# Thresholded attention with a feed-forward layer: sending the thresholds of the first eight pairs through DRAM, with an eighth score buffer and new planner ranks

## The chip, the cores and the metric

The kernel runs on one core of one Trainium2 chip. Its engines are TensorE (PE in the profile, with PEld for weight loads), VectorE (DVE), ScalarE (ACT), GpSimd (POOL) and SyncE (SP), which here only issues DMAs. The metric is the device time of one execution in microseconds; less is better. A change counts as faster or slower from 2%.

## The reference, cut to what matters

```python
# q, k, v: (8 batches, 8 heads, 576 positions, 64); tau = 0.02
scores = scale * np.matmul(q, k.transpose(0, 1, 3, 2))
thresh = np.max(scores, axis=-1, keepdims=True) - tau
scores = np.where(scores >= thresh, scores, -1e9)
attn = softmax(scores)                 # with 1e-9 added to the sum
x = (attn @ v) as (4608 tokens, 512)
h = x @ w_in                           # 512 -> 2048
out = (h * sigmoid(1.702 * h)) @ w_out # 2048 -> 512
```

The weights arrive as 8-byte floats, and the kernel turns them into 4-byte ones itself, in 32 pieces of 0.5 MB, each loaded twice.

## The kernel before

Two heads of one batch are a pair; there are 32. Keys lie on the partitions and queries along the row, so the maximum over keys is taken across partitions. DVE does this in steps: maxima over groups of 32 rows, then over tiles, then over groups. What is left are 2 x 576 = 1152 thresholds, lying as 32 partitions x 36 numbers. The kernel spreads them over 128 partitions (1377 ns) before it subtracts them:

```python
    def lower(n):                       # thresholds of pair n
        f = work.tile([P, 2 * QB], FP32, name="thr", tag="thr")
        nc.vector.tensor_scalar(out=f[0:32], in0=stats[n, ALU.max][0:32],
            scalar1=scl[0:32], scalar2=tau_b[0:32], op0=ALU.mult, op1=ALU.subtract)
        for w in (32, 64):
            nc.vector.tensor_copy(out=f[w : 2 * w], in_=f[0:w])
        stats[n, ALU.max] = f

    def spread_max(n):                  # every threshold on all partitions
        mb = home(n, "mb", 2 * S, "mb", 1)
        nc.vector.transpose(
            out=mb, in_=stats[n, ALU.max].unsqueeze(2).to_broadcast([P, 2 * QB, 32]))
        ...
    def sub(n, t):                      # score * scale - threshold
        ...
            nc.vector.scalar_tensor_tensor(
                out=s, in0=s, scalar=scl, in1=mb, op0=ALU.mult, op1=ALU.subtract)
        ...                             # the tail tile: two such, 64 partitions each
    def exps(n, t):
        nc.scalar.activation(out=s, in_=s, func=AF.Exp, bias=shift)
```

The order of instructions on each engine is made while the kernel is built: every piece of work is a task with an engine, a cost, a rank and a lag until its result can be used, and a planner in the kernel runs them through these figures. The engines then keep to that order and wait where a result is late: DVE's instructions up to 130 us, 131 of them in the trace of the change, stand in the same order in e1 below, with 66.5 us of waits on thresholds in one and 24.1 in the other. A wrong cost gives no wrong result (e4 changes two and is correct), only an order that does not fit the chip.

## Time and profile before

| | before |
|---|---|
| time, median | 1448.8 us (3 runs), 1447.7 with a fourth beside the change |
| profiled span | 1446.5 us |
| PE busy | 1384.0 us |
| DVE busy | 997.7 us |
| last wait of PE | ends at 292.6 us |

PE is the engine that sets the end. It has holes only before 293 us, while DVE is full there; the prediction shows these lines. Two lines that it leans on without showing them come from the page's list of loads (bytes of one issue, then the median time from issue to landing) and from the groups of instructions (count, busy time, mean ns, idle before):

```profile
k_raw<-in_k_dram SPq DMA_DIRECT2D x116, 72.0 KB, 2.3
```

```profile
L411 ACT ACTIVATE s_m<-s_m,shift 128x1152 f32<-128x1152 f32 x120 | 150.2, 1252 | 2.5
```

The first is a load of 576 runs of 128 bytes that lands 2.3 us after the start of its issue (landing times are counted from there throughout). The second is the exponential on a main tile. Two more measurements of this trace, for the prediction. After PE's wait of 9.7 us its granted clock was 0.50 until 29 us and 1.00 from 30 us, and the first three groups of eight matmuls took 2.19, 2.17 and 1.45 us instead of 1.14 to 1.19, about 2.3 us more in all; the same count gives 3.1, 1.6 and 2.8 us after the waits of 4.0, 7.2 and 10.5 us. After the one of 9.4 us the clock was 0.50 until 295.6 us, about 1.5 us lost (an estimate from that clock). And with the weight pieces on their way, the DMA moved 387 to 430 GB/s between 26 and 36 us.

### The profile page before, as it was taken

How to read it: one execution, taken by the hardware profiler on the slowest of the kernel's cores; microseconds unless marked ns; L12 is line 12 of the kernel's file. 1: busy time of each engine (PE TensorE's matmuls, PEld its weight loads, DVE VectorE, ACT ScalarE, POOL GpSimd, SP SyncE). 2: the span in 40 equal slices, each digit the busy share in tenths (PEclk: the TensorE clock that was granted, in tenths of full speed). 3: DMA queues.
4: the chain of work that ended last, by engine and by line, in shares of the span. 5: the costliest groups of instructions: out<-in, count | busy, mean ns of one | idle time of the engine just before them, and what ended most of it. 6: DMA issues, size and time to landing. Idle time of an engine off the chain costs nothing.

```text
span 1446.5 us, 13628 instructions
## 1 busy us (share of the span) xinstructions
PE 1384.0 (96%) x4936; PEld 650.1 (45%) x4936; DVE 997.7 (69%) x1650; ACT 643.6 (44%) x885; POOL 1.3 (0%) x13
## 2 busy tenths in 40 slices
PE   5769979899999999999999999999999999999998
PEld 3334434344444444444444444444444444444443
DVE  7998998888978888888878886788777820200100
ACT  5675544555545554555555554455445500100100
POOL 0000000000000000000000000000000000000000
PEclk8879999999999999999999999999999999999999
DMA  8239461111122012211111111111110000000000
GB/s 240 49 130 287 146 251 40 40 25 25 27 44 49 15 29 39 47 32 25 25 40 39 25 25 39 40 25 21 32 36 16 1 7 22 0 7 22 0 7 22
DMA packets 205074, 72.18 MB, mean 50 GB/s; under 512 B 192208, under 2 KB 192208, under 8 KB 205008
## 3 DMA queue, kind: packets, MB, share of 16 engines
q1 hardware_dynamic: 202640, 71.03, 19.1%
q8 instruction: 39, 0.64, 0.2%
q10 hardware_dynamic: 2368, 0.30, 0.1%
q14 instruction: 27, 0.22, 0.1%
HBM read 61.85 MB, written 9.44 MB: 49 GB/s over the span
## 4 chain that ended last, share of the span: by engine, by line
PE 88%; DVE 8%; ACT 1%; DMA 1%; issue 1%; DVEq 0%; ACTq 0%; SPq 0%
PE ops L523 33%; PE hps L504 31%; PE pv L425 11%; PE ps L319 9%; PE ps L312 2%; PE den L425 2%; DVE part L352 1%; DVE s_m L394 1%; DMA w64s<-in_moe_w_out_dram 1%; DVE mb L386 1%; DVE gT L515 0%; DVE w_out L284 0%; DVE w64s L276 0%; DVE part_t L352 0%; ACT s_m L338 0%
## 5 line engine op out<-in xcount | busy, mean ns | idle before, releaser
L523 PE MATMUL ops<-w_out,gT 128*128 128x512 f32 x1152 | 507.0, 597 | 7.4 <-DVE w_out L284 7.3
L504 PE MATMUL hps<-xT,w_in 128*128 128x512 f32 x1152 | 507.6, 596 | 1.5 <-DVE gT L515 1.4
L352 DVE TRANSPOSE_TENSOR_REDUCE part<-s_m 128x36 f32<-128x1152 f32 x228 | 301.3, 1355 | 107.4 <-ACT s_m L338 106.5
L523 PEld LDWEIGHTS ops<-w_out,gT 128*128 128x128 f32 x1152 | 217.7, 191 | 278.6 <-issue 265.7
L504 PEld LDWEIGHTS hps<-xT,w_in 128*128 128x128 f32 x1152 | 215.3, 190 | 274.2 <-issue 244.4
L515 DVE SCALAR_TENSOR_TENSOR gT<-th,hps 128x512 f32<-128x512 f32 x144 | 97.2, 675 | 226.4 <-ACT th L512 225.8
L338 ACT COPY s_m<-ps 128x576 f32<-128x576 f32 x240 | 137.2, 657 | 144.5 <-PE ps L319 143.3
L407 ACT ACTIVATE s_m<-s_m 128x1152 f32<-128x1152 f32 x120 | 138.4, 1153 | 119.7 <-DVE s_m L394 119.6
L512 ACT ACTIVATE th<-hps 128x512 f32<-128x512 f32 x144 | 85.3, 592 | 229.6 <-PE hps L504 229.5
L394 DVE SCALAR_TENSOR_TENSOR s_m<-s_m,scl,mb 128x1152 f32<-128x1152 f32 x120 | 163.3, 1411 | 0.6
L319 PE MATMUL ps<-qkT 64*128 64x288 f32 x960 | 141.8, 433 | 17.3 <-DVE qkT L295 17.3
L411 ACT ACTIVATE s_m<-s_m,shift 128x1152 f32<-128x1152 f32 x120 | 150.2, 1252 | 2.5
L425 PE MATMUL pv<-s_m,v_m 128*64 128x288 f32 x960 | 126.2, 414 | 0.0
L319 PEld LDWEIGHTS ps<-qkT 64*128 64x128 f32 x960 | 83.2, 190 | 89.4 <-issue 40.4
L530 ACT ACTIVATE osb<-ops 128x512 f32<-128x512 f32 x36 | 21.3, 591 | 220.4 <-PE ops L523 220.4
L425 PEld LDWEIGHTS pv<-s_m,v_m 128*64 128x64 f32 x960 | 67.5, 139 | 64.2 <-issue 15.0
L400 DVE SCALAR_TENSOR_TENSOR s_t<-s_t,scl,mb 64x576 f32<-64x576 f32 x60 | 48.7, 812 | 0.4
L492 DVE TENSOR_TENSOR xT<-pv,rc 128x288 f32<-128x288 f32 (+8 forms) x96 | 28.4, 351 | 22.4 <-PE pv L425 21.1
L352 DVE TRANSPOSE_TENSOR_REDUCE part_t<-s_t 128x18 f32<-128x576 f32 x59 | 43.7, 741 | 0.0
L386 DVE STREAM_TRANSPOSE mb<-thr 128x1152 f32<-128x1152 f32 x30 | 41.3, 1377 | 0.9
L312 PE MATMUL ps<-qkT,kd 128*128 128x288 f32 x120 | 37.1, 432 | 0.0
L425 PE MATMUL pv<-s_t,v_t 128*64 128x288 f32 x256 | 36.5, 406 | 0.0
(66 smaller groups left out, 571.1 us busy)
## 6 DMA issues: line engine op xcount, KB each, us to landing
out_dram<-osb SPq DMA_DIRECT2D x36, 256.0 KB, 2.0
q_raw<-in_q_dram SPq DMA_DIRECT2D x120, 72.0 KB, 2.3
k_raw<-in_k_dram SPq DMA_DIRECT2D x116, 72.0 KB, 2.3
v_m<-in_v_dram SPq DMA_DIRECT2D x64, 128.0 KB, 2.4
w_out<-in_moe_w_in_dram SPq DMA_DIRECT2D x12, 512.0 KB, 6.5
w<-in_moe_w_out_dram SPq DMA_DIRECT2D x12, 512.0 KB, 5.0
w_out<-in_moe_w_in_dram SPq DMA_DIRECT2D x12, 511.6 KB, 7.4
w64s<-in_moe_w_out_dram SPq DMA_DIRECT2D x12, 511.6 KB, 6.0
```

Source lines behind the costliest of these rows:

```text
L312: nc.tensor.matmul(ps[:, i, 0:SH], lhsT=kd[n % 2], rhs=qT[:, ts(i, SH)], start=True, stop=True,)
L319: nc.tensor.matmul(ps[:, h, 0:SH], lhsT=kT[ts(h, D), ts(t, P)], rhs=qT[ts(h, D), ts(c, SH)], start=True, stop=True,)
L338: nc.scalar.copy(out=o, in_=pss.pop((n, t, c))[:, :, 0:SH])
L352: nc.vector.tensor_reduce(out=o, in_=i, axis=AXL.X, op=op, apply_transpose=True)
L394: nc.vector.scalar_tensor_tensor(out=s, in0=s, scalar=scl, in1=mb, op0=ALU.mult, op1=ALU.subtract)
L407: nc.scalar.activation(out=s, in_=s, func=AF.Prelu, alpha=STEEP)
L411: nc.scalar.activation(out=s, in_=s, func=AF.Exp, bias=shift)
L425: nc.tensor.matmul(o[c][ts(h, D), 0:SH], lhsT=lhsT, rhs=rhs, start=(t == 0), stop=(t == NKT),)
L504: nc.tensor.matmul(hidden[j], lhsT=w_in[:, c, ts(j, P)], rhs=xTs[blk][:, c, :], start=(c == 0), stop=(c == NDC - 1),)
L512: nc.scalar.activation(out=ths[j], in_=hidden[j], func=AF.Tanh, scale=GELU_SCALE / 2)
L515: nc.vector.scalar_tensor_tensor(out=gT[j], in0=ths.pop(j), scalar=1.0, in1=hidden.pop(j), op0=ALU.add, op1=ALU.mult)
L523: nc.tensor.matmul(acc[i], lhsT=gT[j][:, ts(i, P)], rhs=w_out[:, j, :], start=(j == 0), stop=(j == NFC - 1),)
```

## The change

The intent is to take work off DVE while DVE holds everything up. For the first eight pairs the 1152 thresholds go to DRAM and come back spread over the partitions by the DMA. The scale moves into the exponential, so that the subtraction becomes a plain one. An eighth buffer of scores and ranks by kind of task let two pairs alternate, so that there is other work while a threshold travels.

```diff
+    EARLY = {"lower": -1.16, "values": 0.42, "exps": 0.63, "load_qk": -0.91, "prep": -1.45}
+    LATER = {"in_groups": 1.11}
     def task(engine, cost, rank, f, *a, after=(), take=(), give=(), lag=0.06):
+        if 0 <= rank < LAST:
+            rank += (EARLY if a[0] < 2 * NPAIR else LATER).get(f.__name__, 0.0)
 ...
     def lower(n):
-            out=f[0:32], in0=stats[n, ALU.max][0:32], scalar1=scl[0:32],
-            scalar2=tau_b[0:32], op0=ALU.mult, op1=ALU.subtract,
-        for w in (32, 64):
+            out=f[0:32], in0=stats[n, ALU.max][0:32], scalar1=gap[0:32], scalar2=None,
+            op0=ALU.subtract,
+        for w in (32, 64) if n >= BY_DMA else ():
 ...
+    def row_out(n):
+        rows[n] = dram.tile([1, 2 * S], FP32, name="row", tag="row", bufs=2)
+        nc.sync.dma_start(
+            out=rows[n].rearrange("o (c i) -> i (o c)", i=32), in_=stats[n, ALU.max][0:32])
+    def row_in(n):
+        ...
+        nc.sync.dma_start(out=mb, in_=row.to_broadcast([P, 2 * S]))
+        for h in range(2):
+            nc.sync.dma_start(out=mbt[ts(h, D)], in_=row[:, ts(h, S)].to_broadcast([D, S]))
 ...
     def sub(n, t):
-            nc.vector.scalar_tensor_tensor(
-                out=s, in0=s, scalar=scl, in1=mb, op0=ALU.mult, op1=ALU.subtract)
+            nc.vector.tensor_tensor(out=s, in0=s, in1=mb, op=ALU.subtract)
+        elif n in mbts:
+            nc.vector.tensor_tensor(out=s, in0=s, in1=mbts.pop(n), op=ALU.subtract)
 ...
-        nc.scalar.activation(out=s, in_=s, func=AF.Exp, bias=shift)
+        nc.scalar.activation(out=s, in_=s, func=AF.Exp, scale=scl, bias=shift)
 ...
+    BY_DMA = 8
 ...
+        if n < BY_DMA:
+            a = task("SP", 0.5, r, row_out, n, after=[a], take=("row",), lag=2.4)
+            m = task("SP", 1.4, r, row_in, n, after=[a], ..., lag=3.2)
```

(Cut: s_m buffers 7 to 8 and, to make room, io 3 to 2 and others by one; tau loaded by GpSimd's queue; one early exponential so that its table is loaded first; adjusted planner costs; ranks of the weight loads.)

More of the change, by code (lines that the diff above doesn't have):

```diff
@@ L22 @@
 EPS = 1e-9
+BIG = 3.0e38
 STEEP = 1.0e30
@@ L79 @@
     work = ctx.enter_context(tc.tile_pool(name="work", bufs=2))
+    dram = ctx.enter_context(
+        tc.tile_pool(name="dram", bufs=2, space=bass.MemoryType.DRAM)
+    )
     psA = ctx.enter_context(tc.tile_pool(name="psA", bufs=3, space=bass.MemoryType.PSUM))
@@ L92 @@
     tau_b = const.tile([P, 1], FP32, name="tau_b")
+    neg = const.tile([P, 1], FP32, name="neg")
     scl = const.tile([P, 1], FP32, name="scl")
+    gap = const.tile([P, 1], FP32, name="gap")
     shift = const.tile([P, 1], FP32, name="shift")
     tasks = []
-    limits = {"psA": 3, "psM": 2, "s_m": 7, "s_t": 2, "io": 3, "xT": 3, "mb": 1,
-              "raw0": 1, "raw1": 1, "qkT0": 1, "qkT1": 1, "v_m": 2, "w64": 2}
+    limits = {"psA": 3, "psM": 2, "s_m": 8, "s_t": 2, "io": 2, "xT": 3, "mb": 1,
+              "raw0": 1, "raw1": 1, "qkT0": 1, "qkT1": 1, "v_m": 2, "w64": 2, "mbt": 1, "row": 2}
     for x in ("raw0", "raw1", "qkT0", "qkT1", "mb"):
@@ L110, in task @@
         return len(tasks) - 1
+    FIRST, LAST = -9.0, 1000.0
     def run_in_order():
@@ L287, in cv_end @@
         )
-    mats, sT, stats, mbs, pss = {}, {}, {}, {}, {}
+    mats, sT, stats, mbs, mbts, rows, pss = {}, {}, {}, {}, {}, {}, {}
     def prep(n, which):
@@ L331, in keep @@
             if c == 0:
-                st = home(n, "s_m", 2 * S, "s_m", 7, f"s_m{t}")
+                st = home(n, "s_m", 2 * S, "s_m", 8, f"s_m{t}")
                 st = st.rearrange("p (h s) -> p h s", h=2)
@@ L344, in in_groups @@
                 work.tile([P, NKT, 2 * QB], FP32, name="part", tag="part", bufs=2),
-                work.tile([P, QB], FP32, name="part_t", tag="part_t", bufs=3),
+                work.tile([P, QB], FP32, name="part_t", tag="part_t", bufs=2),
             ]
@@ L356, in over_tiles @@
         pm, pt = stats[n, op]
-        r = work.tile([P, 2 * QB], FP32, name="red", tag="red", bufs=3)
+        r = work.tile([P, 2 * QB], FP32, name="red", tag="red", bufs=2)
         nc.vector.tensor_reduce(
@@ L367, in over_groups @@
         r = stats[n, op]
-        o = work.tile([64, 2 * QB], FP32, name="fold", tag="fold")
+        o = work.tile([64, 2 * QB], FP32, name="fold", tag="fold", bufs=1)
         for w in (64, 32):
@@ L389, in spread_max @@
         mbs[n] = mb.rearrange("p (h s) -> p h s", h=2)
+    def row_out(n):
+        rows[n] = dram.tile([1, 2 * S], FP32, name="row", tag="row", bufs=2)
+        nc.sync.dma_start(
+            out=rows[n].rearrange("o (c i) -> i (o c)", i=32), in_=stats[n, ALU.max][0:32]
+        )
+    def row_in(n):
+        mb = home(n, "mb", 2 * S, "mb", 1)
+        mbt = work.tile([P, S], FP32, name="mbt", tag="mbt", bufs=1)
+        row = rows.pop(n)
+        nc.sync.dma_start(out=mb, in_=row.to_broadcast([P, 2 * S]))
+        for h in range(2):
+            nc.sync.dma_start(out=mbt[ts(h, D)], in_=row[:, ts(h, S)].to_broadcast([D, S]))
+        mbs[n] = mb.rearrange("p (h s) -> p h s", h=2)
+        mbts[n] = mbt
     def sub(n, t):
@@ L393, in sub @@
         if t < NKT:
-            nc.vector.scalar_tensor_tensor(
-                out=s, in0=s, scalar=scl, in1=mb, op0=ALU.mult, op1=ALU.subtract
-            )
+            nc.vector.tensor_tensor(out=s, in0=s, in1=mb, op=ALU.subtract)
+        elif n in mbts:
+            nc.vector.tensor_tensor(out=s, in0=s, in1=mbts.pop(n), op=ALU.subtract)
         else:
             for h in range(2):
-                x = s[ts(h, D)]
-                nc.vector.scalar_tensor_tensor(
-                    out=x, in0=x, scalar=scl[ts(h, D)], in1=mb[ts(h, D), h, :],
-                    op0=ALU.mult, op1=ALU.subtract,
+                nc.vector.tensor_tensor(
+                    out=s[ts(h, D)], in0=s[ts(h, D)], in1=mb[ts(h, D), h, :], op=ALU.subtract
                 )
@@ L473, in spread_sums @@
         nc.vector.reciprocal(out=r, in_=r)
-        rc = work.tile([P, S], FP32, name="rc", tag="rc")
+        rc = work.tile([P, S], FP32, name="rc", tag="rc", bufs=1)
         nc.vector.transpose(out=rc, in_=r.unsqueeze(2).to_broadcast([P, QB, 32]))
@@ L510, in tanh @@
     def tanh(j):
-        ths[j] = work.tile([P, BLK], FP32, name="th", tag="io", bufs=3)
+        ths[j] = work.tile([P, BLK], FP32, name="th", tag="io", bufs=2)
         nc.scalar.activation(out=ths[j], in_=hidden[j], func=AF.Tanh, scale=GELU_SCALE / 2)
@@ L528, in half @@
     def half(i):
-        osbs[i] = work.tile([P, d_model], FP32, name="osb", tag="io", bufs=3)
+        osbs[i] = work.tile([P, d_model], FP32, name="osb", tag="io", bufs=2)
         nc.scalar.activation(out=osbs[i], in_=acc.pop(i), func=AF.Copy, scale=0.5)
@@ L536 @@
     NP = B * NPAIR
-    nc.sync.dma_start(
-        out=tau_b, in_=bass.AP(tensor=tau.tensor, offset=tau.offset, ap=[[0, P], [1, 1]])
-    )
+    nc.gpsimd.memset(rebias, -896.0 * 2.0**23)
     for t in kd + v_t + [ones_t]:
@@ L543, with first_act @@
     nc.gpsimd.memset(ones, 1.0)
-    nc.gpsimd.memset(rebias, -896.0 * 2.0**23)
     for h in range(2):
         nc.gpsimd.memset(ones_t[ts(h, D), h, :], 1.0)
+    nc.gpsimd.dma_start(
+        out=tau_b, in_=bass.AP(tensor=tau.tensor, offset=tau.offset, ap=[[0, P], [1, 1]])
+    )
+    def first_act():
+        nc.scalar.activation(out=neg, in_=rebias, func=AF.Exp)
     def tau_terms():
+        nc.vector.tensor_single_scalar(out=neg, in_=tau_b, scalar=0.0, op=ALU.is_lt)
         nc.vector.tensor_scalar(
-            out=scl, in0=tau_b, scalar1=0.0, scalar2=SCALE, op0=ALU.is_ge, op1=ALU.mult
+            out=scl, in0=neg, scalar1=-SCALE, scalar2=SCALE, op0=ALU.mult, op1=ALU.add
         )
@@ L558, in tau_terms @@
         nc.vector.tensor_single_scalar(out=shift, in_=tau_b, scalar=-1.0, op=ALU.mult)
-    FIRST, LAST = -1.0, 1000.0
+        nc.vector.tensor_single_scalar(out=gap, in_=tau_b, scalar=1.0 / SCALE, op=ALU.mult)
+        nc.vector.scalar_tensor_tensor(
+            out=gap, in0=neg, scalar=BIG, in1=gap, op0=ALU.mult, op1=ALU.add
+        )
     BY_PE = 5
+    BY_DMA = 8
     LEAD = 6
@@ L568 @@
     for i in range(len(pieces)):
-        rank = NPAIR - 0.4 + 0.5 * i / n_in if i < n_in else NPAIR - 0.16 + 0.9 * (i / n_in - 1)
+        rank = 4.36 + 0.21 * i / n_in if i < n_in else 4.6 + 0.19 * (i / n_in - 1)
         if not wide:
@@ L575 @@
         a = task("SP", 1.1, rank, load_w, i, take=place, lag=5.0)
-        e = task("DVE", 0.44, rank, cv_ex, i, after=[a])
-        m = task("ACT", 0.72, rank, cv_power, i, after=[e])
+        e = task("DVE", 0.43, rank, cv_ex, i, after=[a])
+        m = task("ACT", 0.79, rank, cv_power, i, after=[e])
         a = task("DVE", 1.14, rank, cv_frac, i, after=[e])
         over = [ready_w[y] for y in range(i) if i >= n_in and stage(y) == (i - n_in) // PER_STAGE]
-        ready_w.append(task("DVE", 0.72, rank, cv_end, i, after=[a, m] + over, give=place))
-    tau_done = task("DVE", 1.0, -2.0, tau_terms)
+        ready_w.append(task("DVE", 0.7, rank - 0.47, cv_end, i, after=[a, m] + over, give=place))
+    warm = task("ACT", 1.5, -2.0, first_act)
+    tau_done = task("DVE", 1.0, -2.0, tau_terms, after=[warm])
     placed, ffn = {}, []
@@ L598, in feed_forward @@
                 ffn.append(task(
-                    "PE", 1.79, LAST, mm1, blk, j, p, after=after,
+                    "PE", 1.762, LAST, mm1, blk, j, p, after=after,
                     take=("psM",) if p == 0 else (), give=("xT",) if last else (),
@@ L603, in feed_forward @@
             gelus[j] = task(
-                "DVE", 0.7, FIRST, gelu, j, after=[a, last_mm2.get(j // 2)],
+                "DVE", 0.69, FIRST, gelu, j, after=[a, last_mm2.get(j // 2)],
                 give=("psM", "io"),
@@ L613, in feed_forward @@
                 ffn.append(task(
-                    "PE", 1.79, LAST, mm2, i, p, after=after, take=("psM",) if p == 0 else (),
+                    "PE", 1.762, LAST, mm2, i, p, after=after, take=("psM",) if p == 0 else (),
                 ))
@@ L628 @@
         r = float(n)
+        slow = 1.2 if n < NPAIR else 1.0
         q0, q1 = (nc.sync, nc.scalar) if n == 0 else (nc.sync, nc.sync)
@@ L632 @@
         lv = task("SP", 2.1, r - 1.2, load_v, n, take=("v_m",), lag=2.0)
-        pq = task("DVE", 0.78, r, prep, n, 0, after=[lq], take=own(n, "qkT0"), give=own(n, "raw0"))
-        pk = task("DVE", 0.78, r, prep, n, 1, after=[lk], take=own(n, "qkT1"), give=own(n, "raw1"))
+        pq = task("DVE", 0.77, r, prep, n, 0, after=[lq], take=own(n, "qkT0"), give=own(n, "raw0"))
+        pk = task("DVE", 0.77, r, prep, n, 1, after=[lk], take=own(n, "qkT1"), give=own(n, "raw1"))
         pd = task("ACT", 0.5, r, prep_kd, n, after=[pk])
@@ L642 @@
                 a = task(
-                    "PE", 1.1 if tail else 0.58, r, scores, n, t, c,
+                    "PE", (0.97 if tail else 0.53) * slow, r, scores, n, t, c,
                     after=[pq, pk] + ([pd] if tail else []) + after,
@@ L648 @@
                 after = [a]
-                copies.append(task("ACT", 0.64, r, keep, n, t, c, after=[a], give=("psA",)))
-            mx.append(task("DVE", 0.78 if tail else 1.37, r, in_groups, n, t, ALU.max, after=copies))
-        a = task("DVE", 0.75, r, over_tiles, n, ALU.max, after=mx)
-        a = task("DVE", 0.75, r, over_groups, n, ALU.max, after=[a])
-        a = task("DVE", 0.6, r, lower, n, after=[a, tau_done])
-        m = task("DVE", 1.38, r, spread_max, n, after=[a], take=own(n, "mb"))
+                copies.append(task("ACT", 0.65, r, keep, n, t, c, after=[a], give=("psA",)))
+            mx.append(task("DVE", 0.76 if tail else 1.37, r, in_groups, n, t, ALU.max, after=copies))
+        a = task("DVE", 0.78, r, over_tiles, n, ALU.max, after=mx)
+        a = task("DVE", 0.78, r, over_groups, n, ALU.max, after=[a])
+        a = task("DVE", 0.25 if n < BY_DMA else 0.6, r, lower, n, after=[a, tau_done])
+        if n < BY_DMA:
+            a = task("SP", 0.5, r, row_out, n, after=[a], take=("row",), lag=2.4)
+            m = task(
+                "SP", 1.4, r, row_in, n, after=[a], take=own(n, "mb") + ("mbt",), give=("row",),
+                lag=3.2,
+            )
+        else:
+            m = task("DVE", 1.38, r, spread_max, n, after=[a], take=own(n, "mb"))
         ws, subs = [], [m]
@@ L658 @@
             a = task(
-                "DVE", 1.5 if tail else 1.37, r, sub, n, t, after=subs[-1:],
-                give=own(n, "mb") if tail else (),
+                "DVE", (0.76 if n < BY_DMA else 1.5) if tail else 1.36, r, sub, n, t, after=subs[-1:],
+                give=own(n, "mb") + (("mbt",) if n < BY_DMA else ()) if tail else (),
             )
             subs.append(a)
-            a = task("ACT", 0.7 if tail else 1.17, r, mask, n, t, after=[a])
-            ws.append(task("ACT", 0.88 if tail else 1.36, r, exps, n, t, after=[a]))
+            a = task("ACT", 0.68 if tail else 1.16, r, mask, n, t, after=[a])
+            ws.append(task("ACT", 0.87 if tail else 1.34, r, exps, n, t, after=[a]))
         back = own(n, "s_m") * NKT + ("s_t",)
@@ L672 @@
                 den = task(
-                    "PE", 1.1, r, sums_by_pe, n, [t], True, after=[ws[t], den],
+                    "PE", 1.1 * slow, r, sums_by_pe, n, [t], True, after=[ws[t], den],
                     take=("psM", "psM") if first else (),
@@ L676 @@
                 pv = task(
-                    "PE", 1.1, r, values, n, [t], after=[ws[t], den, pv, lv],
+                    "PE", 1.1 * slow, r, values, n, [t], after=[ws[t], den, pv, lv],
                     take=("psA",) if first else (), give=(back[t],) if t < NKT else ("s_t", "v_m"),
                 )
-            a = task("DVE", 1.2, r, one_row, n, after=[den], give=("psM", "psM"))
+            a = task("DVE", 1.22, r, one_row, n, after=[den], give=("psM", "psM"))
         else:
-            pv = task("PE", 5.0, r, values, n, every, after=ws + [lv], take=("psA",), give=("v_m",))
+            pv = task("PE", 4.85, r, values, n, every, after=ws + [lv], take=("psA",), give=("v_m",))
         if NPAIR <= n < BY_PE:
             a = task("PE", 5.2, r, sums_by_pe, n, every, False, after=ws + [pv], take=("psA",), give=back)
-            a = task("DVE", 1.2, r, one_row, n, after=[a], give=("psA",))
+            a = task("DVE", 1.22, r, one_row, n, after=[a], give=("psA",))
         elif n >= BY_PE:
             su = [
-                task("DVE", 0.78 if t == NKT else 1.37, r, in_groups, n, t, ALU.add, after=[ws[t]])
+                task("DVE", 0.76 if t == NKT else 1.37, r, in_groups, n, t, ALU.add, after=[ws[t]])
                 for t in range(NKT + 1)
             ]
-            a = task("DVE", 0.75, r, over_tiles, n, ALU.add, after=su + [pv], give=back)
-            a = task("DVE", 0.75, r, over_groups, n, ALU.add, after=[a])
+            a = task("DVE", 0.78, r, over_tiles, n, ALU.add, after=su + [pv], give=back)
+            a = task("DVE", 0.78, r, over_groups, n, ALU.add, after=[a])
             a = task("DVE", 0.7, r, one_group, n, after=[a])
-        a = task("DVE", 1.05, r, spread_sums, n, after=[a])
+        a = task("DVE", 1.07, r, spread_sums, n, after=[a])
         b, hp = divmod(n, NPAIR)
@@ L699 @@
         placed[n] = task(
-            "DVE", 0.9, r, place_x, n, after=[a, pv], take=("xT",) * len(new), give=("psA",)
+            "DVE", 1.1, r, place_x, n, after=[a, pv], take=("xT",) * len(new), give=("psA",)
         )
```

## The prediction

> **What bounds the kernel now.** I read the page first: busy shares and the 40 slices.
>
> ```profile
> PE 1384.0 (96%) x4936; PEld 650.1 (45%) x4936; DVE 997.7 (69%) x1650; ACT 643.6 (44%) x885; POOL 1.3 (0%) x13
> ...
> PE   5769979899999999999999999999999999999998
> ...
> DVE  7998998888978888888878886788777820200100
> ...
> PEclk8879999999999999999999999999999999999999
> ```
>
> PE is 96% busy; its holes lie in the first eight slices (about 36 us each), where DVE stands at 8 to 9 tenths and the PE clock is low. From slice 9 on PE is full, so nothing saved there on DVE can move the end; a microsecond saved before about 300 us can. The span holds 1446.5 - 1384.0 = 62.5 us without PE work. The waits of PE say whose they are:
>
> ```profile
> PE ps L319 <- DVE qkT L295: 17.3, 2, 9.4
> PE den L425 <- ACT s_m L411: 16.9, 2, 9.7
> PE den L425 <- ACT gT L411: 14.5, 2, 10.5
> PE ops L523 <- DVE w_out L284: 7.3, 2, 6.3
> ```
>
> These four are 56.0 us; 4 us more is the last store. The timeline places them: 7.95 us of start, 9.7 at 25 us, 4.0 at 55, 7.2 at 75, 10.5 at 103, 7.3 at 209 to 216, 9.4 at 283 to 293, and none later. The waits on ScalarE are only the next link: the exponential waits for the subtraction, which waits for DVE's in-order chain (group maxima, threshold, spread, subtraction). The table of windows confirms that DVE is the bound there:
>
> ```profile
> 20.00:40.00 20.00, 14.57 (x96) 8.03 (x96) 18.88 (x27) 15.00 (x20) 0.00 (x0) 0.75 0.95 332
> ...
> 60.00:80.00 20.00, 12.84 (x92) 6.87 (x88) 18.73 (x32) 10.67 (x11) 0.00 (x0) 0.81 0.07 15
> ...
> 280.00:300.00 20.00, 10.61 (x54) 5.41 (x54) 18.36 (x28) 12.83 (x15) 0.00 (x0) 0.74 0.22 43
> ```
>
> (columns: window, length, busy PE, PE weight load, DVE, ACT, POOL, clock, DMA share, GB/s). DVE is busy 18.4 to 18.9 of 20 us, PE 10.6 to 14.6.
>
> [...] The trace has no such shape, but its two-tensor multiply takes 452 ns at 288 columns and 180 at 32, 1.06 ns a column, which extends to about 1370 and 757[...]. [...] the trace has 2.1 to 2.4 us for small loads on a quiet queue. [...] after the 9.7 us wait eight passes took 2.19 us, warm ones 1.14[...].
>
> **The change part by part.** The DVE rows that it touches (busy us, mean ns, idle before):
>
> ```profile
> L394 DVE SCALAR_TENSOR_TENSOR s_m<-s_m,scl,mb 128x1152 f32<-128x1152 f32 x120 | 163.3, 1411 | 0.6
> ...
> L400 DVE SCALAR_TENSOR_TENSOR s_t<-s_t,scl,mb 64x576 f32<-64x576 f32 x60 | 48.7, 812 | 0.4
> ...
> L386 DVE STREAM_TRANSPOSE mb<-thr 128x1152 f32<-128x1152 f32 x30 | 41.3, 1377 | 0.9
> ...
> L381 DVE COPY thr<-thr 64x36 f32<-64x36 f32 x32 | 5.6, 176 | 1.1
> L381 DVE COPY thr<-thr 32x36 f32<-32x36 f32 x32 | 5.5, 173 | 1.1
> ```
>
> Per pair of the first eight DVE loses the spread 1.38, two copies 0.35, one of two tail subtractions with its scalar (2 x 0.812 - 0.76 = 0.86) and 4 x 0.05 = 0.2 on the main ones: 2.8 us, 22 us for eight pairs. Pairs 8 to 31 save only about 0.3 us each beneath a full PE: nothing. The scale moves into the exponential's own operand, free by the equal form of that row (1252 ns).
>
> It adds to each of those pairs a round trip: scatter of 1152 four-byte elements to DRAM, wait, one read spread over 128 partitions (590 KB) and two for the tail (295 KB). Estimate from the trace's 2.1 to 2.4 us landings and about 400 GB/s for big loads: 0.5 issue + 2.6 landing, 0.3 + 3.2 for the read: 6.6 us of latency, against 1.8 us on DVE. So DVE must have 6.6 us of other work in between. The built order shows what stands there: after pair 0's threshold two transposes and four group maxima of pair 1 (6.9 us); after pair 1's, 5.5; pair 2's, 6.2; pair 3's, 5.2; pair 4's, 7.3; pair 5's, 5.9; pair 6's, 5.4; pair 7's, 5.5. That is why an eighth score buffer and the new ranks come with it: two pairs now alternate. Each pair then leaves DVE waiting about 0.5 to 1.5 us.
>
> Two are worse, because loads now share a queue with thresholds. Before, the timeline of SP's queue (start, length) and the list of loads from 20 to 140 us (median time to landing last):
>
> ```profile
> 29.12 5.58 SPq L189 DMA_DIRECT2D gT<-in_q_dram  x4
> 34.80 4.99 SPq L189 DMA_DIRECT2D gT<-in_k_dram  x4
> ```
>
> ```profile
> gT<-in_q_dram SPq DMA_DIRECT2D x4, 72.0 KB, 8.6
> ```
>
> A 72 KB load issued behind six weight pieces took 8.6 us to land instead of 2.3. In the new order pair 0's row stands behind the q and k loads of pairs 1 to 3 (some 2.1 us of issue each; queue free at about 21.4 us, threshold ready at 19): mb lands near 28, DVE waits 2 us. Pair 1's row stands behind the same six pieces (12 DMAs, 6.1 MB, 15.7 us at 390 GB/s), which now start at about 30 us and drain to 46: threshold ready at 37, row landed 48.5, mb at 52, DVE's other work done at 42. I expect a DVE wait of nearly 10 us there.
>
> Adding DVE durations in the new order with these waits: pair 1's subtraction 52 us, pair 2's 82, pair 3's 96, pair 3's result placed (first feed-forward) 116 us; before, 117.5 by the timeline. The 11 us that four pairs save pay for the waits, and pair 4's scores, prepared early (7 us of DVE, 5.5 us of PE), replace 7 us of weight conversion. From there DVE runs in step with PE: last conversion at 210 us, where by the PE order 15 instructions of the first second-layer group are done as before at 216.4, but pair 6's scores are done too. So the lead is 6.4 + 5.5 = 11.9 us. Then the 9.4 us wait at 283 us: in the new order pair 8's q and k are ready about 2 us after PE asks for them (275.5 against 273.6), so some 7 us and the cold clock after it (1 to 2) go as well. PE then goes on without a hole from 281 us with 9 pairs scored, 8 with values, 64 first-layer and 64 second-layer steps done.
>
> The sum, in PE work from warm rows (a feed-forward step 54.93/64 = 0.858 us, values 5.0 and scores 5.5 a pair): all work 988.7 + 160 + 25 + 176.6 = 1350, plus 12 that the same count misses before[...]: 1362. Done by 281 us: 49.5 + 40 + 25 + 109.8 = 224. End: 281.2 + 1138 + 3.7 = 1423 us. The same sum for before (294.8 us, 215 done) gives 1445 against 1446.5. Timed runs are 2 us above the span: 1425.
>
> The start changes little: tau no longer holds up q (0.4 us), the exponential's table (1.28 us at 7.98 us before) is loaded while loads fly, but k's issue waits behind it; about 1 us won at the first group maximum, which pair 0's queue wait eats. Smaller io, red, fold and rc buffers are in-order on DVE or limited by two PSUM buffers anyway; I count nothing.
>
> **The rivals.** *A: the round trip is slower (four-byte writes).* [...] 128-byte ones took little here (576 landed in 2.3 us). With 2 us more per trip DVE waits 2 us more in each of eight pairs, most of it before 210 us: about 1437. *B: the weights do not delay pair 1's row* (the drain is faster[...]): the 10 us wait falls to 1 or 2 and the chain of DVE up to 210 us moves with it: 1415. *C: nothing is won, because PE, full from 300 us, sets the end.* Against it: PE's holes lie before and cost the end one for one. *D: DVE idles more from 116 to 210 us*, where conversion waits for buffers; there were 7 us of it before and I counted almost none: 1430.
>
> **Range and chances.** 1425 us; A and D above, B below: 1409 to 1441. Two per cent is 1419.8, half a deviation away: faster 0.33, same 0.65, slower 0.02.
>
> **What would show it.** Spread and copies gone from eight pairs and subtraction rows of about 1.36 and 0.76 us; the first feed-forward at 116 us; DVE idle on a DMA of about 10 us near 42 to 52 us and under 2 us for the other pairs; PE's waits before 120 us nearly as long as before but fewer, the one at 283 us down to about 2. It is wrong if pair 1's row lands soon (B), if the waits on mb are 3 us each (A), or if new PE holes appear after 300 us.

## The result, and the profile after

The changed kernel took 1480.9 us (median of 4 runs, 1479.5 to 1482.2) against 1447.7 us of the kernel before (median of 4). The ratio is 1.0228, with an interval of 1.0211 to 1.0246. Here and below a ratio is the mean time of a kernel's fast runs over that of the runs of the kernel before that go with them, so it is not quite the ratio of the medians that I quote. The change is slower by over 2%; I had predicted 1425 us (1409 to 1441) and given slower a chance of 0.02.

First the page's slices, now of 37 us each:

```profile
PE   4467798969999999999999999999999999999998
...
DVE  6577687778899888778877787777877740110200
...
PEclk8789899989999999999999999999999999999999
```

In the first eight slices PE's holes are deeper than before, and DVE, which stood at 7 to 9 tenths there, now stands at 5 to 8. DVE has less to do and is no longer full: it waits. The waits of PE (total, times, longest) and those of DVE on a DMA:

```profile
PE den L455 <- ACT gT L441: 26.0, 6, 17.2
PE den L455 <- ACT s_m L441: 24.8, 4, 12.6
PE ps L334 <- DVE qkT L310: 12.5, 4, 8.5
```

```profile
DVE s_m L426 <- DMA mb<-row: 42.5, 6, 10.2
DVE gT L426 <- DMA gT<-row: 24.0, 2, 16.8
```

The first two lines were 14.5 and 16.9 us before; the same link, the exponential, stands in front of PE. Behind it DVE's subtractions stand still for 42.5 + 24.0 = 66.5 us until the spread thresholds have come back (gT is the place of pairs 1 and 3, mb that of the others). Eight waits, one for each pair. I had counted about 17 us: 2 for pair 0, nearly 10 for pair 1, and 4.8 for the other six, which is what the prediction's list of other work leaves of 6.6 us. The list of loads says which half of the trip is long:

```profile
mb<-row SPq DMA_DIRECT2D x6, 576.0 KB, 4.6
...
gT<-row SPq DMA_DIRECT2D x2, 576.0 KB, 4.2
...
row<-thr SPq DMA_DIRECT2D x8, 4.5 KB, 7.5
```

The 4.5 KB that go out take 7.5 us to land, longer than the 576 KB that come back. On the page's chain of work that ended last, these writes alone (row<-thr) are 4% of the span, some 60 us; mb<-row is 2% and gT<-row 1%. The timeline of SP's queue shows pairs 0 and 1 (start, length of the issue):

```profile
21.09 0.44 SPq L409 DMA_DIRECT2D row<-thr  x1
28.24 0.35 SPq L417 DMA_DIRECT2D mb<-row  x1
...
45.63 0.33 SPq L409 DMA_DIRECT2D row<-thr  x1
58.30 0.33 SPq L417 DMA_DIRECT2D gT<-row  x1
```

The read is issued as soon as the write has landed. For pair 0 that is 7.15 us after its issue; for pair 1, behind the weight pieces, 12.7 us. DVE's timeline has the other end, with the idle time before each first subtraction in brackets:

```profile
32.13 5.16 DVE L426 TENSOR_TENSOR s_m<-s_m,mb 128x1152 f32<-128x1152 f32 x4 [5.23 <-DMA mb<-row]
...
62.37 2.63 DVE L426 TENSOR_TENSOR gT<-gT 128x1152 f32<-128x1152 f32 x2 [16.79 <-DMA gT<-row]
...
99.10 5.16 DVE L426 TENSOR_TENSOR s_m<-s_m,mb 128x1152 f32<-128x1152 f32 x4 [9.09 <-DMA mb<-row]
```

The prediction had 28, 52 and 82 us in these three places. The single instructions came out as worked out, but for one:

```profile
L426 DVE TENSOR_TENSOR s_m<-s_m,mb 128x1152 f32<-128x1152 f32 x120 | 156.2, 1352 | 43.2 <-DMA mb<-row 42.5
...
L428 DVE TENSOR_TENSOR s_t<-s_t,mbt 128x576 f32<-128x576 f32 x8 | 6.0, 750 | 0.0
```

```profile
L441 ACT ACTIVATE s_m<-s_m,shift,scl 128x1152 f32<-128x1152 f32 x120 | 160.3, 1343 | 2.6
```

The subtractions take 1352 and 750 ns (estimated about 1370 and 757 from the rows of the multiply). The exponential takes 1343 ns, not 1252. DVE's busy time fell by 27.5 us, from 997.7 to 970.2, near the 29 that the parts add up to (22 for eight pairs, 0.3 for each of the other 24). So DVE's work is saved, and the waits take more than it saves. They reach further than before, too: PE now has four waits of 1.8 to 3.2 us that end between 311 and 328 us, where it had none. New holes after 300 us were one of the signs of being wrong that the prediction names.

### The profile page after: what moved, and what is told of

It reads as the page before. It is cut to its first block, busy times and chain, and to the rows that moved or that the text cites. A ratio compares the mean times of both kernels' runs of the same rounds, so it can differ in the third digit from the quotient of the medians.

```text
span 1480.4 us, 13694 instructions
## 1 busy us (share of the span) xinstructions
PE 1388.1 (94%) x4936; PEld 650.7 (44%) x4936; DVE 970.2 (66%) x1621; ACT 660.8 (45%) x886; POOL 2.0 (0%) x14
## 4 chain that ended last, share of the span: by engine, by line
PE 82%; DMA 8%; DVE 7%; ACT 1%; issue 1%; SPq 1%; DVEq 0%; ACTq 0%
PE hps L534 33%; PE ops L553 30%; PE pv L455 8%; PE ps L334 8%; DMA row<-thr 4%; PE ps L327 2%; DVE part L367 2%; DMA mb<-row 2%; DVE s_m L426 1%; DMA gT<-row 1%; DMA w_out<-in_moe_w_in_dram 1%; DVE part_t L367 0%; DVE gT L426 0%; DVE xT L522 0%; PE den L455 0%
## 5 line engine op out<-in xcount | busy, mean ns | idle before, releaser
L353 ACT COPY s_m<-ps 128x576 f32<-128x576 f32 x240 | 138.6, 652 | 172.4 <-PE ps L334 170.8
L426 DVE TENSOR_TENSOR s_m<-s_m,mb 128x1152 f32<-128x1152 f32 x120 | 156.2, 1352 | 43.2 <-DMA mb<-row 42.5
L441 ACT ACTIVATE s_m<-s_m,shift,scl 128x1152 f32<-128x1152 f32 x120 | 160.3, 1343 | 2.6
L455 PE MATMUL pv<-s_m,v_m 128*64 128x288 f32 x960 | 127.4, 416 | 6.2 <-ACT s_m L441 6.2
L455 PEld LDWEIGHTS pv<-s_m,v_m 128*64 128x64 f32 x960 | 67.5, 139 | 72.5 <-issue 11.2
L455 PE MATMUL den<-s_m,ones 128*64 128x288 f32 x96 | 15.0, 457 | 24.8 <-ACT s_m L441 24.8
L455 PE MATMUL den<-gT,ones 128*64 128x288 f32 x64 | 12.8, 535 | 26.0 <-ACT gT L441 26.0
L455 PE MATMUL pv<-s_t,v_t 128*64 128x288 f32 x256 | 36.5, 406 | 0.0
```

Source lines behind the costliest of these rows:

```text
L353: nc.scalar.copy(out=o, in_=pss.pop((n, t, c))[:, :, 0:SH])
L426: nc.vector.tensor_tensor(out=s, in0=s, in1=mb, op=ALU.subtract)
L441: nc.scalar.activation(out=s, in_=s, func=AF.Exp, scale=scl, bias=shift)
L455: nc.tensor.matmul(o[c][ts(h, D), 0:SH], lhsT=lhsT, rhs=rhs, start=(t == 0), stop=(t == NKT),)
```

## The experiments

Three theories at the start. S: the scatter of 1152 four-byte elements makes the row land in 7.3 us, and the rest of the reasoning holds. O: the new order itself (ranks, alternating pairs) is what costs. R: any two DMAs in a row cost this much, or the read does. The runs were made on three chips; the kernel before, run on each beside them, took 1447.7, 1447.2 and 1447.5 us (medians), so rows of different chips can be compared. Times are medians.

| run | what | time us | ratio to before (95%) | DVE waits on the row, us |
|---|---|---|---|---|
| after | the change | 1480.9 | 1.0228 (1.0211 to 1.0246) | 66.5 |
| e1_contig | row written in long runs (wrong result) | 1434.9 | 0.9912 (0.9894 to 0.9929) | 24.1 |
| e2_no_dma | all thresholds spread by DVE | 1434.9 | 0.9911 (0.9896 to 0.9926) | none |
| e3_turned | row turned on DVE first | 1437.1 | 0.9921 (0.9906 to 0.9935) | 21.4 |
| e4_true_lag | planner told the true latency | 1482.8 | 1.0240 (1.0223 to 1.0257) | 70.9 |
| e5_pool | turned, GpSimd's queue | 1452.3 | 1.0034 (1.0016 to 1.0053) | 32.7 |
| e6_hold | turned, weights held back | 1423.6 | 0.9837 (0.9822 to 0.9852) | 9.0 |
| e7_runs8 | runs of 8 bytes (wrong result) | 1463.1, one run | - | 50.1 |
| e8_old_ranks | as e2, without the ranks | 1441.0 | 0.9955 (0.9938 to 0.9971) | none |
| e9_fixed_scale | as e6, scale a constant | 1423.1 | 0.9834 (0.9821 to 0.9847) | 7.2 |
| e10_dma_old_ranks | the change without the ranks | 1485.1 | 1.0258 (1.0244 to 1.0272) | 56.6 |
| e11_hold_scatter | scatter, weights held back | 1476.4 | 1.0198 (1.0184 to 1.0211) | 61.2 |

The last column adds the two lines of DVE waits that end on the row read back.

### e1_contig: the same order, long runs

```diff
-            out=rows[n].rearrange("o (c i) -> i (o c)", i=32), in_=stats[n, ALU.max][0:32]
+            out=rows[n].rearrange("o (i c) -> i (o c)", i=32), in_=stats[n, ALU.max][0:32]
```

The thresholds land in the wrong places, so the result is wrong (relative error 0.56). Every compute engine has the same instructions in the same order as in the change.

> Wrong results on purpose: the threshold row is written to DRAM as 32 contiguous runs of 144 bytes instead of 1152 scattered elements of 4 bytes; the order on every compute engine is that of the changed kernel, instruction for instruction. Theory S (the scatter itself makes the row take 7.3 us to land instead of the 2.6 us that I had put down): the row lands in 2 to 2.5 us on a quiet queue, each of the eight DVE waits on the spread row shrinks by about 5 us (66 us in all to 25 to 30, pair 1 still over 10), and the time falls from 1481 to 1435 to 1450. Theory O (the new ranks and the alternation of two pairs are what costs): the waits move elsewhere and the time stays above 1465. Theory R (it is the read back, 4.2 us, [...] not the scatter): the row still takes over 5 us to land and the time stays above 1470.

It took 1434.9 us, 46 us less than the change. How long the eight writes took to land, from the trace of that instruction, and DVE's waits on the rows:

```profile
DMA to landing us min/median/max: 1.3/2.1/9.0
```

```profile
DVE gT L426 <- DMA gT<-row: 14.9, 2, 14.7
...
DVE s_m L426 <- DMA mb<-row: 9.2, 5, 3.5
```

The median landing falls from 7.5 to 2.1 us, and the waits from 66.5 to 24.1 us. 42.4 us of DVE waits less gave 46 us of time, so the waits go into the end one for one and a little more. The rest goes with PE's clock: between the two profiled executions, 49.3 us apart, PE's idle time fell by 42.8 us and its busy time for the same matmuls by 6.5 (1388.1 to 1381.6), with a mean granted clock of 0.988 instead of 0.974. S holds; O and R fall, because the order and both DMAs are still there. Pair 1's wait of 14.7 us stays: that one is not the scatter.

### e2_no_dma: everything but the DRAM trip

```diff
-    BY_DMA = 8
+    BY_DMA = 0
```

> The changed kernel with the number of pairs that go through DRAM set to 0: all thresholds are spread by DVE as before, while the eighth buffer, the new ranks, the plain subtraction and the smaller buffers stay (the planner rearranges some instructions). Theory S: nothing waits on a DMA for thresholds, DVE does about 20 us more work than in the changed kernel; 1435 to 1455, about as before. Theory O: 1465 or more, clearly slower than before although no threshold goes through DRAM.

1434.9 us: 46 us faster than the change, and 13 us faster than the kernel before. The planner rearranges some instructions, so this is not the same order. It says that the rest of the change is a gain and the DRAM trip, as built, a loss.

### e3_turned: a correct mend

```diff
+        if n < BY_DMA:
+            nc.vector.transpose(out=f[32:64, 0:32], in_=f[0:32, 0:32])
+            nc.vector.transpose(out=f[64:96, 0:32], in_=f[0:32, 2 * QB - 32 : 2 * QB])
 ...
-        nc.sync.dma_start(
-            out=rows[n].rearrange("o (c i) -> i (o c)", i=32), in_=stats[n, ALU.max][0:32])
+        q, f = 2 * QB - 32, stats[n, ALU.max]
+        by_c = rows[n].rearrange("o (c i) -> c (o i)", i=32)
+        nc.sync.dma_start(out=by_c[0:32], in_=f[32:64, 0:32])
+        nc.sync.dma_start(out=by_c[32 : 32 + q], in_=f[96 - q : 96, 0:32])
```

The row in DRAM is the same as in the change, so the result is correct. It leaves as 36 runs of 128 bytes, in two DMAs of 32 and 4.

> A correct mend: two 32x32 transposes on DVE[...] turn the thresholds before they leave, so that the row goes to DRAM as 36 runs of 128 bytes in two DMAs; the order is otherwise that of the changed kernel. Theory S: as the contiguous row, plus some 0.5 us per pair for the transposes and for a second DMA issue: 1440 to 1455. Theory O: above 1465. Theory R: above 1470.

1437.1 us, a little below the band that I gave. The transposes took 0.20 us each, and the larger write landed in 1.9 us (the trace gives one such landing, of pair 4). This confirms S without a wrong result. But it is no faster than e2, which does all on DVE: against e2 the trip saves 15.6 us of DVE's busy time (989.2 to 973.6) and adds 21.4 us of waits.

### e4_true_lag: can the planner work around it?

```diff
-            a = task("SP", 0.5, r, row_out, n, after=[a], take=("row",), lag=2.4)
+            a = task("SP", 0.5, r, row_out, n, after=[a], take=("row",), lag=6.8)
```

(and row_in from 3.2 to 3.3.)

> The scatter stays; only the planner's figure for it changes, from 2.4 us to 6.8 us after the issue, so that the planner itself puts more work between a threshold and its subtraction. If the loss is one of planning with a wrong latency, part of the 66 us of DVE waits is filled with other work: 1455 to 1470. If the order has no other work to offer in the first 120 us (four pairs, two of them alive at a time), it stays within 8 us of 1481.

1482.8 us, no better. The planner's wrong figure is not the reason by itself: told one near the measured (the writes of this run landed in 8.0 us, median), it finds nothing to put there with these buffers and ranks. DVE's waits on rows even rose, from 66.5 to 70.9 us.

### e7_runs8: what the landing time goes with

```diff
-            out=rows[n].rearrange("o (c i) -> i (o c)", i=32), in_=stats[n, ALU.max][0:32]
+            out=rows[n].rearrange("o (c i j) -> i (o c) j", i=32, j=2),
+            in_=stats[n, ALU.max][0:32].rearrange("i (c j) -> i c j", j=2),
```

Wrong result; the same bytes in 576 runs of 8.

> Wrong results on purpose: the row is written as 576 runs of 8 bytes instead of 1152 of 4, all else as in the changed kernel. If the time to land goes with the number of runs (1152: 7.3 us, 32: 2.1 us, so about 4.6 ns each): about 4.7 us on a quiet queue, and a time near 1455. If any run that short costs the same in all (a penalty that does not go with their number), 7 us and 1480; if only runs below 8 bytes are slow, 2.5 us and 1437.

```profile
DMA to landing us min/median/max: 3.7/4.5/10.8
```

The median is 4.5 us, between 2.1 us for 32 runs and 7.5 us for 1152; a straight line through these two gives 4.7. So the time fits the number of short runs written, near 4.8 ns each ((7.5 - 2.1)/1120): 4.4 ns for each further run from 32 to 576 ((4.5 - 2.1)/544), 5.2 from 576 to 1152 ((7.5 - 4.5)/576). The loads of q and k have 576 runs too and land in 2.3 us, so the figure is one for tiny runs written to DRAM and not for every run. Whether the size or the direction makes them slow was not separated. The one time, 1463 us, of unknown state, lies between the other two and a little above my 1455.

### e5_pool: another queue

```diff
-        nc.sync.dma_start(...)        # in row_out and row_in
+        nc.gpsimd.dma_start(...)
-            a = task("SP", 0.5, r, row_out, ...
+            a = task("POOL", 0.5, r, row_out, ...
```

(on top of e3_turned, and row_in likewise.)

> The turned row (36 runs of 128 bytes, correct), written and read back through GpSimd's queue instead of SyncE's, so that neither stands behind weight pieces in the same queue. Theory Q (pair 1's wait of 13.5 us in the turned version is its place behind 6 MB of weights in one queue): pair 1's DVE wait falls below 6 us and the time from 1437 to 1424 to 1431. Rival ([...]the row waits for the weights anyway): the wait of pair 1 stays above 10 us and the time within 4 us of 1437.

1452.3 us, slower than e3 by 15 us. Neither side was right. DVE's first subtractions of pairs 1 and 4:

```profile
50.80 1.36 DVE L430 TENSOR_TENSOR gT<-gT 128x1152 f32<-128x1152 f32 x1 [6.58 <-DMA gT<-row]
...
141.03 1.36 DVE L430 TENSOR_TENSOR s_m<-s_m,mb 128x1152 f32<-128x1152 f32 x1 [9.21 <-DMA mb<-row]
```

Pair 1's wait is halved, from 13.5 to 6.6 us, so the place in the queue did matter. But pair 3, which waited 0.3 us in e3, waits 6.8, and pair 4, which waited 3.2, waits 9.2: its read was issued at 130.6 us and landed at 141.0. The row itself landed in 1.8 us (median of the larger write), as from SyncE's queue; but for pair 4 the read could be issued only 5.2 us after the row's issue, and the median landing of pairs 1 and 3's reads was 7.2 us, not 4.2 as in the change. That rows and weights then move side by side, and that SyncE, which is no longer stopped at each threshold, issues weights further ahead, was my guess from the order of issues; no run isolates it. The order also changed with the planner's new engine, so this run says only that another queue, by itself, is no mend.

### e6_hold: thresholds before weights

```diff
+        loads_w.append(a)             # the task of each weight load
 ...
+            if n == 1:                # m: pair 1's thresholds are read back
+                for w in loads_w:
+                    tasks[w][5].append(m)
```

(on top of e3_turned; all on SyncE's queue.)

> The turned row, and the planner holds all weight loads back until pair 1's threshold has been read back; all stays on SyncE's queue. Theory Q: pair 1's wait falls to under 2 us, the weights arrive 10 us later but before their first use on DVE: 1420 to 1428, what I had predicted for the change itself. Rival (what is won on pair 1 is lost again, because conversion or the first feed-forward now waits for weights): 1432 or more, with DVE waits on weight loads.

DVE's waits on the rows, in e3 and then here:

```profile
DVE gT L430 <- DMA gT<-row: 13.8, 2, 13.5
...
DVE s_m L430 <- DMA mb<-row: 7.6, 4, 3.2
```

```profile
DVE s_m L430 <- DMA mb<-row: 8.8, 4, 3.7
...
DVE gT L430 <- DMA gT<-row: 0.2, 1, 0.2
```

1423.6 us, ratio 0.9837: 1.6% faster than the kernel before (under the 2% from which a change counts here) and 3.9% faster than the change (1423.6/1480.9). Pair 1's wait is gone (the 0.2 us are pair 3's); no DVE wait on a weight load appears. 12.4 us less waiting than in e3 gave 13.5 us of time. This is the best version that uses tau as given; it is correct. Of the 9.0 us of waits that are left, 3.7 each are pairs 2 and 4, and the timelines show why: their rows are issued 3.8 and 4.8 us after the threshold is ready, behind loads of q and k in the same queue. Holding those back as well was not tried.

### e11_hold_scatter: the second half of the mend alone

The same hold on the unmended change, with its scatter.

> The changed kernel with the 4-byte scatter, but weight loads held back until pair 1's threshold is read back: the second half of the mend alone. Pair 1's DVE wait falls from 16.8 us to the 5 to 7 us of a scatter on a quiet queue, so if the two losses simply add: 1466 to 1472 (the mended row gained 14 us from this hold). If with the slower scatter the weights come too late: over 1475.

1476.4 us: 4.5 us less than the change (the two intervals just touch), where the hold gave 13.5 us with the turned row. DVE's first subtractions of pairs 1 and 2:

```profile
52.17 2.63 DVE L426 TENSOR_TENSOR gT<-gT 128x1152 f32<-128x1152 f32 x2 [6.12 <-DMA gT<-row]
...
91.31 5.17 DVE L426 TENSOR_TENSOR s_m<-s_m,mb 128x1152 f32<-128x1152 f32 x4 [11.49 <-DMA mb<-row]
```

Pair 1's wait shrinks by 10.7 us (16.79 to 6.12), but pair 2's grows from 9.1 to 11.5 us (its row is issued 4.3 us after its threshold, not 3.0, and takes 8.8 us to land, not 7.3) and pair 4's stays at 10 us. The two losses do not simply add. My lower expectation was too good. The time fell into the band of the other one, weights that come too late, but not for its reason: DVE's only wait on a weight load is 1.1 us.

### e8_old_ranks and e10_dma_old_ranks: what the ranks do

```diff
-            rank += (EARLY if a[0] < 2 * NPAIR else LATER).get(f.__name__, 0.0)
+            rank += 0.0
```

e8 has this on top of e2_no_dma, e10 on the change.

> No threshold through DRAM (all spread by DVE) and the ranks by kind of task taken out too: what is left of the change is the eighth buffer, plain subtraction, smaller buffers, the start and the planner's costs. The version with ranks and without DRAM took 1435, 13 us less than before. If the ranks are what wins there: 1443 to 1450. If the eighth buffer and the rest win: 1432 to 1438.

> The changed kernel, scatter and all, without the ranks by kind of task. My prediction took the ranks to be what gives DVE work during the round trip. If so, this is clearly slower than the change: over 1490. If the planner fills the trip as well without them, and they only bring the 6 us that they bring without DRAM: 1481 to 1489. If they hurt with a slow trip: under 1478.

e8 took 1441.0 us, e10 1485.1 us. Without DRAM the ranks are worth 6 us (1441.0 - 1434.9), with the scatter about 4 us (1485.1 - 1480.9; the two intervals just overlap). So they neither cause the loss nor are they what hides the trip: the planner puts other work there without them as well (DVE's waits on rows are 56.6 us in e10, even less than in the change; but there PE waits 15.5 us for ScalarE's copies of scores, L353, before matmuls of L455, which it does not in the change). What is left, e8 against before, is 6 us; it contains the eighth buffer, the plain subtraction, the start, the smaller buffers and the adjusted planner costs, and these were not taken apart.

### e9_fixed_scale: the longer exponential

```diff
-        nc.scalar.activation(out=s, in_=s, func=AF.Exp, scale=scl, bias=shift)
+        nc.scalar.activation(out=s, in_=s, func=AF.Exp, scale=SCALE, bias=shift)
```

(on top of e6_hold; right for tau that is not negative, as here.)

> The best version so far (turned row, weights held back: 1423.6 us), with the exponential's scale given as a constant instead of as a column of scl; right for this tau only, otherwise the same order. The changed kernel's exponential takes 1343 ns against 1252 before, although both read 128x1152. If the column for the scale is what costs the 91 ns: 1252 ns again, and since some of PE's waits before 120 us end on the exponential, 1420 to 1423. If the row is longer for another reason[...]: it stays at 1343 and the time does not move.

```profile
L445 ACT ACTIVATE s_m<-s_m,shift 128x1152 f32<-128x1152 f32 x120 | 149.6, 1254 | 2.5
```

1254 ns again: the column given as scale is what costs the 90 ns. The time, 1423.1 us, is that of e6 within the intervals, so in e6 this cost lies beside other work; on the change itself it was not tried.

## Why the prediction was wrong

**What bounds the kernel: right.** PE's holes before 300 us (in the change, before 330) set the time, and DVE's chain sets the holes. In e1, e3, e6 and e7, with an order nearly or wholly the same, time moved with DVE's waits by 1.0 to 1.1 us for each: 42.4 us to 46 from the change to e1, 45.1 to 43.8 from the change to e3, which also adds transposes, 12.4 to 13.5 from e3 to e6. Rival C, nothing to be won, is answered by e6, 24 us faster than the kernel before.

**The DVE costs: right.** 1352, 750, 1377 and 173 to 176 ns are the rows that I used or within 20 ns of them. The clause "free by the equal form of that row (1252 ns)" was wrong by 91 ns: the equal form has a column as bias alone, and the change adds one as scale. The traces show what it costs: 1343 ns with the column, 1254 with a constant in e9, 89 ns less. e9 shows that it cost e6 no time that the runs can tell.

**The step that failed: "0.5 issue + 2.6 landing, 0.3 + 3.2 for the read: 6.6 us of latency".** From the start of its issue the write takes 7.5 us to land, not 3.1 (0.5 + 2.6), and the read 4.2 to 4.6, not 3.5 (0.3 + 3.2). (The landings of 2.1 to 2.4 us that I started from already count from the start of the issue, so the sum has the issue twice; without that it would be shorter still.) The trip is about 12 us where 5.2 to 7.3 us of other work stand ready. I took the landing time from loads of 72 KB, which are 576 runs of 128 bytes, and applied it to 1152 runs of 4 bytes written to DRAM, although rival A has the four-byte writes in its name. e1 and e7, with the same bytes in fewer and longer runs (2.1 us for 32, 4.5 us for 576), show that it was the short runs. "128-byte ones took little here" was the wrong comparison: the case had no tiny run to look at, and I let the number of bytes stand for the number of runs.

**Rival A was the true one, and I made it too small.** I allowed 2 us more per trip and 1437 us. It was 4.4 us more for the write and about 1 us for the read. Eight trips of 5.4 us are 43 us, and the waits came out 50 us above my 17 (66.5). About as much as the other 7 us is something that I had not seen at all: in the timelines of the change, the rows of pairs 2 and 4 are issued 3.0 and 4.4 us after their thresholds are ready, because loads of q and k stand before them in SyncE's queue. At 1.1 us of time each, 50 us are 55, and the miss was 1480.9 - 1425 = 56.

**Pair 1 behind the weights: right in kind, too small in size.** I expected nearly 10 us; it was 16.8 us with the scatter and 14.7 us in e1 with the fast row, where the place behind the weights is left. So rival B, no delay there, was wrong. In e1 the row was issued at 42.1 us and landed at 51.1, where I had 48.5, and DVE was done with its other work at 40 us instead of 42. The hold removed it.

**The chain after that: nearly right once the trip was short.** In e1 the subtractions of pairs 1, 2 and 3 start at 55, 85 and 98.5 us (I had 52, 82 and 96), and pair 3's result is placed at 117.7 us (116; before, 117.5). The last conversion ends at 213.5 us (210), and the hole near 281 us is 2.2 us (2). e1 takes 1434.9 us against my 1425; pair 1's 5 us, and 1 to 4 us of waits in pairs 2, 4 and 5, are in that difference. e6, with a short trip and no weights in front, takes 1423.6. That this is close to 1425 is luck: e6 has 9 us of waits where my sum had 17, so by the sum it should have been some 8 us faster (1.1 us of time for each). One thing that the sum lacked is rival D: DVE idle for other reasons from 116 to 210 us, of which I counted almost none. In e1 DVE is idle for 9.9 us of that stretch, 6.4 without its waits on rows, much as the 7.2 before. No run isolates its share.

**The start: wrong by 1.5 us.** I expected 1 us won; the first group maximum started at 11.51 us against 11.01. Tau came by GpSimd's queue 4.1 us after its issue (2.7 before, by SyncE), its six terms stand first on DVE, and the transposes waited behind them until 7.0 us.

**The claim that the ranks make the alternation: not borne out.** e10 shows the waits no longer without them.

## What to carry to other kernels

Before sending a small thing through DRAM, count its contiguous runs, not only its bytes: 4.5 KB in 1152 runs took 7.5 us to land, longer than the 4.2 to 4.6 us of 576 KB read back, and two small transposes of 0.2 us each brought the landing down to 1.9 us. A latency that a schedule is built around deserves a measurement of that very transfer; a similar looking load is not one (2.3 us for 72 KB of q or k). And what travels on a dependent chain should be issued before the bulk loads of the same queue: pair 1's wait of 13.5 us behind the weights in e3 was gone in e6.
